# A layer-norm square root moved from GpSimd to ScalarE, V stores moved to GpSimd's queue, and unread matmuls in the gaps of an opening

## Chip, cores, metric

One core of a Trainium2 chip. The metric is the time of one execution in microseconds (us) on the device; each run is one execution. The core has a matmul engine (PE, with its weight loads PEld), VectorE (DVE), ScalarE (ACT), GpSimd (POOL) and SyncE (SP, which here only issues transfers). Runs come in two states, "fast" and "slow": on one core, a run is counted as slow when it took over 1.5% longer than the fastest run of the same kernel.

## The reference, cut to what matters

```python
def _attn_ref(q, k, v, sort_net):            # 4 batches, 8 heads, 768 rows, 64 columns
    P = sort_net
    for _ in range(5):                       # Sinkhorn: exp and two normalisations
        P = np.exp(P - np.max(P, axis=-1, keepdims=True))
        P = P / (np.sum(P, axis=-1, keepdims=True) + 1e-09)
        P = P / (np.sum(P, axis=-2, keepdims=True) + 1e-09)
    # (lines drawn together) ... keys and values mixed blockwise by P, then softmax attention in each block

def _moe_ref(x, w_ch1, w_ch2):
    mixed = np.real(np.fft.fft(np.fft.fft(x, axis=1), axis=2))
    u = x + mixed
    mu = np.mean(u, axis=-1, keepdims=True)
    var = np.mean((u - mu) ** 2, axis=-1, keepdims=True)
    un = (u - mu) / np.sqrt(var + 1e-06)     # the layer norm of this case
    return u + np.maximum(un @ w_ch1, 0.0) @ w_ch2
```

`x` is the attention output (4 x 768 x 512). Each batch is normalised in two halves of three 128-row tiles: eight normalisations in all.

## The kernel before

The program lists operations with estimated costs and lets a planner decide, before anything runs, in which order each engine takes them and which buffer each uses. So a cost that is wrong in the list gives a wrong order. The parts concerned:

```python
    many("u", 6, [128, DM], F32)
    many("un", 2, [128, DM], F16)
# ... mixed V to DRAM (SP) and back, spread differently (POOL)
                P.add({"SP": (0.4, 4.2)}, lambda _, w64=w64, cols=cols:
                      nc.sync.dma_start(vdr[t][w64, cols], vm[w64, cols]), ...)
                o = P.add({"POOL": (1.3, 1.3)}, ...  nc.gpsimd.dma_start(vsb..., vdr[t]...))
# ... the normalisation: mv holds mean and variance of three tiles
        P.add({"POOL": (0.25, 0.25)}, lambda _: G.tensor_scalar(
            mv.ap[:, :, 1], mv.ap[:, :, 1], 1e-6, None, op0=ALU.add), ...)
        P.add({"POOL": (0.9, 0.9)}, lambda _: G.tensor_tensor(
            ny.ap, mv.ap[:, :, 1], mhalf, op=ALU.pow), ...)          # (var+eps)^-0.5
        P.add({"POOL": (0.2, 0.2)}, ...)                             # nm = mean*ny
        P.add({"POOL": (0.25, 0.25)}, ...)                           # nm = -nm
# ... un = u*ny + nm, on ACT or DVE; batch 0 transposes it on PE, the others by DMA on SP
# ... first MLP layer: 4 matmuls fill a bank, ACT or DVE empties it with a relu into hr
            P.add({"ACT": act(GT), "DVE": dve(GT)}, f, r=[ps], w=[("h", g, fc)], ...)
# ... second layer into a bank; DVE adds it to u; u goes out
                    nc.gpsimd.indirect_dma_start(out..., rows[...], u.ap, None)
            P.add({"SP": (0.1, 2.3)} if g == 0 else {"POOL": (1.2, 3.5)}, f, ..., tag="out")
```

The output rows of the second half of a batch are scattered by a transfer that this kernel issues from GpSimd, and `u` has six buffers, so a later `u` can be written only when such a store has landed.

Names used below: `ex`, exponentials of the attention scores; `vdr`, mixed V in DRAM, and `vsf`, the same gathered back; `rt`, attention output; `rb`, a small operand of the Fourier products, brought in by four transfers on SP; `un` and `ut`, the normalised rows and their transpose; `hr`, an emptied bank of the first MLP layer ("bank" is one of the eight result buffers that the program sets up for PE; the MLP layers use three); `ny` and `nm`, the norm's factor and offset.

The softmax here doesn't subtract the row's maximum and nothing guards it: scores larger than these inputs give would overflow.

Of the kernel before, what the change touches and what calls it, by code (L numbers as in the profile page):

```python
# [25 lines left out]
RSC = 1.0 / XSC  # L26
YSC = 1.0 / 32.0
LOOK = {}
QB = (2, 3)
NK = 193  # L30
TOK = [list(range(1, 129)), list(range(129, 257)),
# [339 lines left out]
def kernel(  # L371
# [63 lines left out]
    many("y", 1, [128, 4, 2 * NK], F16)  # L435
    many("hi", 1, [128, 258], F16)
    many("u", 6, [128, DM], F32)
    many("un", 2, [128, DM], F16)
    many("ut", 2, [128, 4, GT], F16)
    tab = ct("tab", [128, 2, 2, 257], F32)  # L440
    cs = ct("cs", [128, 2, 3, 2 * NK], F16)
# [10 lines left out]
    vbn = ct("vbn", [128, D], F16)  # L452
    rows = ct("rows", [128, 3 * B], mybir.dt.uint32)
    negone = ct("negone", [128, 1], F32)
    mhalf = ct("mhalf", [128, 3], F32)
    mone = ct("mone", [128, 3], F32)
    many("rz", 4, [128, 6], F32)
    many("st", 3, [128, 6], F32)
    many("mv", 2, [128, 3, 2], F32)
# [23 lines left out]
    def load(dst, src, nbytes, w, prio, eng="POOL", r=(), after=()):  # L483
        e = {"POOL": nc.gpsimd, "SP": nc.sync}[eng]
        c = (0.8, 0.8) if eng == "POOL" else (0.1, 2.3)
        o = P.add({eng: c}, lambda _: e.dma_start(dst, src), r=r, w=w,  # L486
                  prio=prio, nbytes=nbytes, tag="load", after=after,
                  behind=gate)
        o.late = 4.0 if after else 0.0
        return o  # L490


    gate = ()
# [32 lines left out]
    def hk(g):  # L526
        return [("h", g, fc) for fc in range(16)]

    def load_v(t, hf, prio):
        if t == 0:  # L530
            load(nat[0][:, 3072 * hf:3072 * hf + 3072].rearrange(
                "p (c d) -> p c d", d=D),
                vv[0:128, 48 * hf:48 * hf + 48, :], 1572864,
                [("nat", 0, hf)] + hk(0)[8 * hf:8 * hf + 8], prio)
            return
        keys = kqk(2 * hf) + kqk(2 * hf + 1)
        past = {o for n in keys for d_ in (P.wr, P.rd) for o in d_.get(n, ())}
        for n in keys:
            P.wr[n], P.rd[n] = [], []
        for r in range(3 * hf, 3 * hf + 3):  # L540
            load(nat[1][:, 1024 * r:1024 * r + 1024].rearrange(
                "p (c d) -> p c d", d=D),
                vv[128:256].rearrange(
                    "p (c r) d -> p r c d", r=6)[:, r], 690000,
                [("nat", 1, r)], prio + 0.01 * r, after=tuple(past))
            P.ops[-1].late = 0.0
            for n in keys:
                P.wr[n].append(P.ops[-1])
# [16 lines left out]
    for n in range(2):  # L565
# [4 lines left out]
        vsb[0:96, :, D:D + 1], 1.0 / XSC), w=["vsz"], prio=-200.0, tag="vsz")  # L570
    P.add({"POOL": (0.1, 0.4)}, lambda _: nc.gpsimd.memset(
        pmt[:, 4:7, DM:DM + 2], 0.0), w=["pmz"], prio=-150.0, tag="small")
    for t_, val in ((negone, -1.0), (mhalf, -0.5), (mone, 1.0)):
        P.add({"POOL": (0.1, 0.4)}, lambda _, t_=t_, val=val:
              nc.gpsimd.memset(t_, val), w=["smalls"], prio=-199.0, tag="small")
    P.add({"POOL": (0.9, 0.9)}, lambda _: nc.gpsimd.tensor_tensor(
        mone, mone, mhalf, op=ALU.pow), r=["smalls"], w=["mone"], prio=-198.0,
        tag="small")

    early = dict(  # L580
        pw=(pw, sort_net.rearrange("b h i j -> (b h) i j"), 8192),
# [167 lines left out]
    def v_mix(t):  # L749
# [27 lines left out]
        for hb in range(2):  # L777
            w64 = slice(64 * hb, 64 * hb + 64)
            for k_ in range(3):
                cols = slice(2048 * k_, 2048 * k_ + 2048)  # L780
                P.add({"SP": (0.4, 4.2)}, lambda _, w64=w64, cols=cols:
                      nc.sync.dma_start(vdr[t][w64, cols], vm[w64, cols]),
                      r=[("vm", t, n) for n in range(4 * k_, 4 * k_ + 4)]
                      + (stage if t else vmk), w=[("vdr", t, k_, hb)],
                      prio=P.prio + 6 * hb, tag="vst")
# [401 lines left out]
    def dft2(b, g):  # L1187
# [11 lines left out]
        for tt in range(3):  # L1199
# [62 lines left out]
                mv.ap[:, tt, :], st.ap), r=[st], w=[(mv, tt)], tag="bna")  # L1262
        ny, nm = Buf("ny"), Buf("nm")
        mvs = [(mv, tt) for tt in range(3)]
        G = nc.gpsimd
        P.add({"POOL": (0.25, 0.25)}, lambda _: G.tensor_scalar(  # L1266
            mv.ap[:, :, 1], mv.ap[:, :, 1], 1e-6, None, op0=ALU.add),
            r=mvs, w=[(mv, 3)], tag="ln")
        P.add({"POOL": (0.9, 0.9)}, lambda _: G.tensor_tensor(
            ny.ap, mv.ap[:, :, 1], mhalf, op=ALU.pow),  # L1270
            r=[(mv, 3), "mone"], w=[ny], tag="ln")
        P.add({"POOL": (0.2, 0.2)}, lambda _: G.tensor_tensor(
            nm.ap, mv.ap[:, :, 0], ny.ap, op=ALU.mult),
            r=[(mv, 3), ny], w=[nm], tag="ln")
        P.add({"POOL": (0.25, 0.25)}, lambda _: G.tensor_scalar(
            nm.ap, nm.ap, -1.0, None, op0=ALU.mult), r=[nm], w=[(nm, 1)],
            tag="ln")
        lns.append(P.ops[-1])
        ut = Buf("ut")
        uts[b, g] = ut  # L1280
        for tt in range(3):
            un, pt, u = Buf("un"), Buf("pf"), us[b, g][tt]

            def f(e, tt=tt, un=un, u=u):
                if e == "ACT":
                    nc.scalar.activation(un.ap, u.ap, AF.Identity,  # L1286
                                         scale=ny.ap[:, tt:tt + 1],
                                         bias=nm.ap[:, tt:tt + 1])
                else:
                    V.tensor_scalar(un.ap, u.ap, ny.ap[:, tt:tt + 1],  # L1290
                                    nm.ap[:, tt:tt + 1],
                                    op0=ALU.mult, op1=ALU.add)
            P.add({"ACT": (0.72, 0.81), "DVE": (0.45, 0.55)}, f,
                  r=[u, ny, (nm, 1)], w=[un], tag="un")
            if b > 0:
                P.add({"SP": (1.3, 4.0)}, lambda _, tt=tt, un=un:
                      nc.sync.dma_start_transpose(
# [141 lines left out]
                -300.0)  # L1439
    with tc.manual_schedule():  # L1440
        P.aim(goal[0])
        for o in P.schedule():
            o.fn(o.eng)
# [1 line left out]
_INS = ['q', 'k', 'v', 'sort_net', 'moe_w_ch1', 'moe_w_ch2']  # L1445
# [26 lines left out]
```

## Time and profile before

| | before |
|---|---|
| median (runs) | 297.19 us (three, 296.29 to 297.81) |
| PE busy | 257.1 us, 88% |
| first MLP matmul | 66.48 us |
| PE between 150 and 250 us | busy all 100 us |
| longest waits of PE after the start | ex 2.6, u 2.5, gathered V 1.6 us |

In the views by line, each row names line, engine, operation and tiles; the brackets at the end of a row say how long the engine had stood idle before it, and who released it.

### The profile page before, as it was taken

The numbers are of one execution on the slowest core, as the hardware profiler recorded it, in microseconds if no ns is written. First come the engines' busy times: TensorE is split into PE (matmuls) and PEld (weight loads), VectorE is DVE, ScalarE is ACT, GpSimd is POOL, SyncE is SP. The second block draws the span as 40 slices with busy tenths as digits, with TensorE's granted clock in tenths as the row PEclk, the third lists the DMA queues.
The fourth block names the chain that finished last, engine by engine and source line by source line (L and its number), as shares of the span: only waits on it lengthen the run. The fifth ranks groups of instructions, "written<-read, shape, count | busy, mean of one in ns | idle before, by whom it ended". The sixth has DMA issues, their size and how long they took to land.

```text
span 293.2 us, 5526 instructions
## 1 busy us (share of the span) xinstructions
PE 257.1 (88%) x2124; PEld 146.9 (50%) x2124; DVE 173.9 (59%) x407; ACT 145.1 (49%) x307; POOL 84.8 (29%) x120
## 2 busy tenths in 40 slices
PE   0698697769999999696999999999999999999980
PEld 0255484465555464453557456456555545545530
DVE  6899879896999997384999452146124315310020
ACT  2289649666642586643697126327514505605400
POOL 8914843049730056830220001023000212200021
PEclk9999759987999999999999999999999999999997
DMA  7999999999996369999303011411311131141001
GB/s 128 202 203 287 217 229 173 213 209 141 164 173 122 80 162 221 170 144 153 92 22 57 2 72 36 56 72 50 56 72 37 36 56 72 36 92 36 0 36 72
DMA packets 56543, 32.60 MB, mean 111 GB/s; under 512 B 42842, under 2 KB 51560, under 8 KB 56516
## 3 DMA queue, kind: packets, MB, share of 16 engines
q0 software_dynamic: 36592, 21.46, 50.6%
q1 hardware_dynamic: 19926, 10.80, 16.8%
q8 instruction: 16, 0.26, 0.4%
q14 instruction: 9, 0.07, 0.1%
HBM read 32.12 MB, written 9.44 MB: 142 GB/s over the span
## 4 chain that ended last, share of the span: by engine, by line
PE 47%; DMA 3%; issue 1%; DVE 1%; POOLq 0%; DVEq 0%
PE bank L1326 21%; PE bank L1347 20%; DMA out_dram<-u,rows 3%; PE bank L1221 1%; PE bank L1133 1%; PE bank L1060 1%; PE bank L1225 1%; PE bank L1021 1%; POOLq L1467 0%; PE bank L966 0%; PE bank L1138 0%; PE bank L1209 0%; DVE u L1355 0%; DVE u L1245 0%; PE bank L1143 0%
## 5 line engine op out<-in xcount | busy, mean ns | idle before, releaser
L1326 PE MATMUL bank<-ut,w1sb 128*128 128x384 f16 x512 | 93.8, 330 | 3.0 <-DVE u L1355 2.8
L1338 ACT ACTIVATE hr<-bank 128x384 f16<-128x384 f32 x109 | 53.3, 490 | 71.1 <-PE bank L1326 70.4
L1347 PE MATMUL bank<-w2sb,hr 128*128 128x512 f16 x384 | 87.8, 379 | 0.0
L1326 PEld LDWEIGHTS <-w1sb 128*128 128x128 f16 x512 | 48.9, 99 | 38.0 <-issue 5.0
L1347 PEld LDWEIGHTS <-hr 128*128 128x128 f16 x384 | 36.9, 98 | 41.7 <-issue 0.2
L1355 DVE TENSOR_TENSOR u<-bank,u 128x512 f32<-128x512 f32 x24 | 16.5, 690 | 54.5 <-PE bank L1347 54.2
L1030 ACT ACTIVATE ex<-bank 96x384 f32<-96x384 f32 x64 | 28.4, 485 | 10.7 <-PE bank L1021 10.2
L1368 POOL DMA_INDIRECT out_dram<-u,rows x12 | 12.1, 1006 | 72.4 <-DVE u L1355 54.4
L1266 POOL TENSOR_SCALAR mv<-mv 128x3 f32<-128x3 f32 x8 | 1.9, 240 | 78.8 <-DVE mv L1261 75.7
L788 POOL DMA_DIRECT2D vsf<-vdr x12 | 13.0, 1088 | 34.8 <-DMA vdr<-kq 23.4
L1060 PE MATMUL bank<-vsf,eb 97*128 97x65 f16 x416 | 18.6, 206 | 2.6 <-DMA vsf<-vdr 1.6
L1060 PEld LDWEIGHTS <-eb 97*128 97x128 f16 x416 | 16.8, 107 | 5.2 <-issue 2.8
L1045 ACT ACTIVATE eb<-ex,negone 96x384 f16<-96x384 f32 x31 | 18.5, 613 | 0.3
L486 POOL DMA_DIRECT2D kq<-in_q_dram x20 | 16.4, 833 | 6.9 <-DMA kq<-in_k_dram 2.1
L1286 ACT ACTIVATE un<-u,nm,ny 128x512 f16<-128x512 f32 x15 | 12.2, 811 | 11.4 <-DMA ut<-un 9.1
L1076 DVE TENSOR_TENSOR rt<-bank,rz 128x384 f16<-128x384 f32 x32 | 17.2, 549 | 0.4
L1245 DVE SCALAR_TENSOR_TENSOR u<-rt,bank 128x510 f32<-128x510 f16 x12 | 8.1, 679 | 15.5 <-DMA out_dram<-u,rows 9.9
L1233 DVE SCALAR_TENSOR_TENSOR u<-rt,bank 128x512 f32<-128x512 f16 x12 | 8.0, 685 | 14.8 <-PE bank L1225 14.8
L1259 DVE BATCH_NORM_STATS2 st<-u 128x6 f32<-128x512 f32 x24 | 16.1, 682 | 0.2
L1021 PE MATMUL bank<-qt,ks 64*128 64x96 f16 x256 | 12.8, 213 | 3.7 <-ACT ex L1030 2.9
L966 PE MATMUL bank<-bdk,kq 128*64 128x128 f16 x192 | 10.6, 228 | 3.4 <-ACT ex L1030 1.5
L694 ACT CAST ks<-bank 128x384 f16<-128x384 f32 x18 | 8.2, 484 | 10.7 <-PE bank L966 10.6
(137 smaller groups left out, 317.3 us busy)
## 6 DMA issues: line engine op xcount, KB each, us to landing
kq<-in_k_dram POOLq DMA_DIRECT2D x8, 384.0 KB, 10.1
vsf<-vdr POOLq DMA_DIRECT2D x12, 256.0 KB, 6.9
w1sb<-in_moe_w_ch_dram POOLq DMA_DIRECT2D x4, 512.0 KB, 16.9
w2sb<-in_moe_w_ch_dram POOLq DMA_DIRECT2D x4, 512.0 KB, 19.3
out_dram<-u SPq DMA_DIRECT2D x8, 256.0 KB, 2.0
hr<-in_v_dram POOLq DMA_DIRECT2D x2, 768.0 KB, 9.4
kq<-in_q_dram POOLq DMA_DIRECT2D x4, 384.0 KB, 13.9
vdr<-hr SPq DMA_DIRECT2D x6, 256.0 KB, 5.0
```

Source lines behind the costliest of these rows:

```text
L486: o = P.add({eng: c}, lambda _: e.dma_start(dst, src), r=r, w=w, prio=prio, nbytes=nbytes, tag="load", after=after, behind=gate)
L788: nc.gpsimd.dma_start(vsb[32 * k_:32 * k_ + 32, w64, 0:D], vdr[t][w64, cols].rearrange("g (c d) -> c g d", d=D)),
L1021: nc.tensor.matmul(pss[h2].ap[:, BLK * j:BLK * j + BLK], ks.ap[rows, 4 * g + j, :], qt.ap[rows, c0:c0 + BLK])
L1030: nc.scalar.activation(ex.ap, pss[h2].ap[0:96, 0:384], AF.Exp, scale=SCALE),
L1045: nc.scalar.activation(ed, src, AF.Identity, bias=negone[0:96])
L1060: nc.tensor.matmul(po.ap[:, 65 * T:65 * T + 65], eb.ap[:, e0:e0 + 128], vsf[:, vi:vi + 65], start=(n == 0), stop=(n == len(WIN[T]) - 1), s ...
L1076: P.add({"DVE": (0.45, 0.56)}, lambda _: V.tensor_tensor(rt.ap[:, :, D * h:D * h + D], po3()[:, :, 0:D], rz.ap[:, :, None].broadcast_to([1 ...
L1259: P.add({"DVE": (0.6, 0.69)}, lambda _, u=u, st=st: V.bn_stats(st.ap, u.ap), r=[u], w=[st], tag="bn")
L1326: nc.tensor.matmul(ps.ap[:, 0:GT], w1sb[:, c, 128 * fc:128 * fc + 128], ut.ap[:, c, :], start=(c == 0), stop=(c == 3))
L1338: nc.scalar.activation(hr[g][:, fc, :], ps.ap[:, 0:GT], AF.Relu)
L1347: nc.tensor.matmul(ps.ap, hr[g][:, fc, 128 * tt:128 * tt + 128], w2sb[:, fc, :], start=(fc == 0), stop=(fc == 15))
L1355: V.tensor_tensor(u.ap, ps.ap, u.ap, op=ALU.add),
```

## The change

The intent: use ScalarE, idle half of the time, for the square root (ln, then exp of minus half of it), free GpSimd and give it the V stores that had stood on SP before the transposes, and keep PE's clock up (0.74 and 0.57 in the two stretches from 29.3 to 44 us before) by matmuls whose result nobody reads. Three parts.

Part A, unread matmuls, planned into gaps until the first layer norm:

```diff
+SPIN = 0.22
+    spin = Buf("pm")
+    P.add({"PE": (0.001, 0.001)}, lambda _: None, w=[spin], prio=-9000.0, tag="spin")
...
         for o in P.schedule():
+            if o.eng == "PE":
+                if o.start < goal[0].end:
+                    for _ in range(int((o.start - t - 0.05) / SPIN)):
+                        nc.tensor.matmul(spin.ap[:, 0:480], idh, pack.bitcast(F16))
+                t = max(t, o.start + o.costs["PE"][0])
             o.fn(o.eng)
```

Part B, stores and one more buffer:

```diff
-    many("un", 2, [128, DM], F16)
+    many("un", 3, [128, DM], F16)
...
-                P.add({"SP": (0.4, 4.2)}, lambda _, w64=w64, cols=cols:
-                      nc.sync.dma_start(vdr[t][w64, cols], vm[w64, cols]),
+                P.add({"POOL": (0.7, 4.5)} if t else {"SP": (0.4, 4.2)},
+                      lambda e, w64=w64, cols=cols:
+                      (nc.gpsimd if e == "POOL" else nc.sync).dma_start(
+                          vdr[t][w64, cols], vm[w64, cols]),
+                      behind=() if t or hb == 0 else gets[0, 0][-1:],
```

Part C, the norm:

```diff
+    P.add({"ACT": (1.5, 1.6)}, lambda _: nc.scalar.activation(
+        mone, eps, AF.Ln), r=["eps"], w=["mone"], prio=-9000.0, tag="small")
...
-        # four operations on POOL: add eps, pow, mult, negate
+        P.add({"ACT": (0.17, 0.24)}, lambda _: nc.scalar.activation(
+            ny.ap, mv.ap[:, :, 1], AF.Ln, bias=eps), ...)
+        P.add({"ACT": (0.17, 0.24)}, lambda _: nc.scalar.activation(
+            ny.ap, ny.ap, AF.Exp, scale=-0.5), ...)
+        P.add({"DVE": (0.08, 0.18)}, lambda _: V.scalar_tensor_tensor(
+            nm.ap, mv.ap[:, :, 0], -1.0, ny.ap, op0=ALU.mult, op1=ALU.mult), ...)
...
-                    V.tensor_scalar(un.ap, u.ap, ny..., nm..., op0=ALU.mult, op1=ALU.add)
+                    V.tensor_scalar(un.ap, u.ap, mv..., ny..., op0=ALU.subtract, op1=ALU.mult)
```

(One more line of the change, a longer assumed landing time of a V load, is left out here.)

More of the change, by code (lines that the diff above doesn't have):

```diff
@@ L454 @@
     negone = ct("negone", [128, 1], F32)
-    mhalf = ct("mhalf", [128, 3], F32)
-    mone = ct("mone", [128, 3], F32)
+    eps = ct("eps", [128, 1], F32)
+    mone = ct("mone", [128, 1], F32)
     many("rz", 4, [128, 6], F32)
@@ L490, in load @@
         return o
+    spin = Buf("pm")
+    P.add({"PE": (0.001, 0.001)}, lambda _: None, w=[spin], prio=-9000.0,
+          tag="spin")
     gate = ()
@@ L534, in load_v @@
                 [("nat", 0, hf)] + hk(0)[8 * hf:8 * hf + 8], prio)
+            P.ops[-1].late = 1.2
             return
@@ L572 @@
         pmt[:, 4:7, DM:DM + 2], 0.0), w=["pmz"], prio=-150.0, tag="small")
-    for t_, val in ((negone, -1.0), (mhalf, -0.5), (mone, 1.0)):
-        P.add({"POOL": (0.1, 0.4)}, lambda _, t_=t_, val=val:
-              nc.gpsimd.memset(t_, val), w=["smalls"], prio=-199.0, tag="small")
-    P.add({"POOL": (0.9, 0.9)}, lambda _: nc.gpsimd.tensor_tensor(
-        mone, mone, mhalf, op=ALU.pow), r=["smalls"], w=["mone"], prio=-198.0,
-        tag="small")
+    P.add({"DVE": (0.06, 0.12)}, lambda _: V.memset(eps, 1e-6), w=["eps"],
+          prio=-9100.0, tag="small")
+    P.add({"POOL": (0.1, 0.4)}, lambda _: nc.gpsimd.memset(negone, -1.0),
+          w=["smalls"], prio=-199.0, tag="small")
+    P.add({"ACT": (1.5, 1.6)}, lambda _: nc.scalar.activation(
+        mone, eps, AF.Ln), r=["eps"], w=["mone"], prio=-9000.0, tag="small")
     early = dict(
@@ L1264, in dft2 @@
         mvs = [(mv, tt) for tt in range(3)]
-        G = nc.gpsimd
-        P.add({"POOL": (0.25, 0.25)}, lambda _: G.tensor_scalar(
-            mv.ap[:, :, 1], mv.ap[:, :, 1], 1e-6, None, op0=ALU.add),
-            r=mvs, w=[(mv, 3)], tag="ln")
-        P.add({"POOL": (0.9, 0.9)}, lambda _: G.tensor_tensor(
-            ny.ap, mv.ap[:, :, 1], mhalf, op=ALU.pow),
-            r=[(mv, 3), "mone"], w=[ny], tag="ln")
-        P.add({"POOL": (0.2, 0.2)}, lambda _: G.tensor_tensor(
-            nm.ap, mv.ap[:, :, 0], ny.ap, op=ALU.mult),
-            r=[(mv, 3), ny], w=[nm], tag="ln")
-        P.add({"POOL": (0.25, 0.25)}, lambda _: G.tensor_scalar(
-            nm.ap, nm.ap, -1.0, None, op0=ALU.mult), r=[nm], w=[(nm, 1)],
-            tag="ln")
+        P.add({"ACT": (0.17, 0.24)}, lambda _: nc.scalar.activation(
+            ny.ap, mv.ap[:, :, 1], AF.Ln, bias=eps), r=mvs + ["eps"],
+            w=[(ny, 0)], tag="ln")
+        P.add({"ACT": (0.17, 0.24)}, lambda _: nc.scalar.activation(
+            ny.ap, ny.ap, AF.Exp, scale=-0.5), r=[(ny, 0)], w=[ny], tag="ln")
+        P.add({"DVE": (0.08, 0.18)}, lambda _: V.scalar_tensor_tensor(
+            nm.ap, mv.ap[:, :, 0], -1.0, ny.ap, op0=ALU.mult, op1=ALU.mult),
+            r=mvs + [ny], w=[nm], tag="ln")
         lns.append(P.ops[-1])
@@ L1289, in f @@
                 else:
-                    V.tensor_scalar(un.ap, u.ap, ny.ap[:, tt:tt + 1],
-                                    nm.ap[:, tt:tt + 1],
-                                    op0=ALU.mult, op1=ALU.add)
+                    V.tensor_scalar(un.ap, u.ap, mv.ap[:, tt, 0:1],
+                                    ny.ap[:, tt:tt + 1],
+                                    op0=ALU.subtract, op1=ALU.mult)
             P.add({"ACT": (0.72, 0.81), "DVE": (0.45, 0.55)}, f,
-                  r=[u, ny, (nm, 1)], w=[un], tag="un")
+                  r=[u, ny, nm] + mvs, w=[un], tag="un")
             if b > 0:
@@ L1441 @@
         P.aim(goal[0])
+        P.add({"PE": (0.001, 0.001)}, lambda _: None, r=[spin],
+              after=[goal[0]], prio=-2000.0, tag="spun")
+        t = 3.5
         for o in P.schedule():
+            if o.eng == "PE":
+                if o.start < goal[0].end:
+                    for _ in range(int((o.start - t - 0.05) / SPIN)):
+                        nc.tensor.matmul(
+                            spin.ap[:, 0:480], idh,
+                            pack.bitcast(F16))
+                t = max(t, o.start + o.costs["PE"][0])
             o.fn(o.eng)
```

## The prediction

> **What bounds the kernel now.** I read the page first: busy shares, then the 40 slices.
>
> ```profile
> PE 257.1 (88%) x2124; PEld 146.9 (50%) x2124; DVE 173.9 (59%) x407; ACT 145.1 (49%) x307; POOL 84.8 (29%) x120
> ...
> PE   0698697769999999696999999999999999999980
> ...
> PEclk9999759987999999999999999999999999999997
> ```
>
> PE sets the end from about 66 us on; before that the opening is a chain through DMA, DVE, ACT and PE. The PEclk row has two dips, in slices 5 to 6 and 9 to 10. The view by stretches gives them sizes:
>
> ```profile
> core 0: us, PE busy (x) PEld busy (x) DVE busy (x) ACT busy (x) POOL busy (x), PEclk, DMA share, GB/s
> 29.30:36.60 7.30, 4.39 (x78) 3.53 (x77) 5.91 (x14) 5.00 (x12) 6.57 (x10) 0.74 1.03 217
> 36.60:44.00 7.40, 7.40 (x109) 6.57 (x106) 5.39 (x18) 3.44 (x8) 3.51 (x6) 0.57 1.21 228
> 58.60:66.00 7.40, 4.93 (x96) 4.50 (x95) 7.26 (x26) 4.51 (x8) 3.06 (x8) 0.83 1.24 209
> 66.00:73.30 7.30, 7.30 (x71) 4.37 (x68) 5.09 (x12) 4.88 (x10) 7.08 (x7) 0.70 1.63 141
> 150.00:200.00 50.00, 50.00 (x387) 28.33 (x382) 26.30 (x65) 22.29 (x48) 6.37 (x11) 1.00 0.19 44
> 200.00:250.00 50.00, 50.00 (x284) 27.32 (x282) 17.85 (x38) 21.75 (x45) 6.19 (x11) 1.00 0.22 55
> ```
>
> The two last rows matter most: from 150 to 250 us PE is busy in all 100 us while ACT is busy in 44. There nothing can be gained by relieving POOL, and whatever stalls PE is added to the end in full. What PE still waits for is in its wait view, and the stall of 2.56 us at 119.6 us is explained by ACT's order of time:
>
> ```profile
> PE bank L1021 <- ACT ex L1030: 2.9, 3, 2.6
> PE bank L1326 <- DVE u L1355: 2.8, 2, 2.5
> ...
> 118.35 0.81 ACT L1286 ACTIVATE un<-u,nm,ny 128x512 f16<-128x512 f32 x1 [3.69 <-DMA ut<-un]
> ```
>
> ACT stood 3.69 us before the third normalised tile (only two "un" buffers), since the transposes that read the first two sat on SP behind six mixed-V stores (8.37 us on SP, from 101.63). The exponentials behind it came late, and PE with them. The second wait is another one: DVE cannot write "u" until an output store issued at 129.70 has landed at about 137.2.
>
> What is removed costs this on POOL, per normalisation (first one):
>
> ```profile
> 59.38 0.25 POOL L1266 TENSOR_SCALAR mv<-mv 128x3 f32<-128x3 f32 x1 [8.82 <-DVE mv L1261]
> 59.71 0.89 POOL L1269 TENSOR_TENSOR ny<-mv,mhalf 128x3 f32<-128x3 f32 x1
> 60.68 0.19 POOL L1272 TENSOR_TENSOR nm<-mv,ny 128x3 f32<-128x3 f32 x1
> 60.96 0.26 POOL L1275 TENSOR_SCALAR nm<-nm 128x3 f32<-128x3 f32 x1
> ```
>
> The last moment is in place on DVE at 59.27 and the normalisation on ACT and DVE starts at 61.25: 1.98 us of latency, and none of it on an engine that anybody needs. The price of its substitute is in the first line of ACT:
>
> ```profile
> 0.72 1.28 ACT L626 ACT_TABLE_LOAD   x1 [0.72 <-PEq L1456]
> 2.95 0.26 ACT L626 ACTIVATE rv<-rv 32x64 f32<-32x64 f32 x1 [0.94 <-DVE rv L623]
> ```
>
> [...] in the order of ACT's instructions a load stands before each ln and another before each exp[...]; 18 loads where there was one. No run shows it yet, but the order is fixed. [...] the first six 512-column matmuls took 2.72 us, the next six 1.46; and the clock is 0.50 in the views of 33 to 41 and 64 to 70 us, after stretches in which PE was about half busy (1.01 of 2.00 us in 31 to 33, 1.14 of 2.00 in 62 to 64). [...]
>
> **The change, part by part.**
>
> Part A, unread matmuls. I count 68 in PE's order, 480 columns each, 0.20 us at full clock (worked out from 512 columns in about 0.216 us in the mixing stage). 34 stand before the first real work and hide behind the loads of V. 19 stand between about 25 and 50 us, 15 around the first normalisation. They keep a bank of the three for the MLP until then, where it is hardly needed. If the clock stays up: from 34.9 to 43 us PE works at half clock (39 attention-times-V matmuls in 2.31 us against about 1.2 at full speed, the 16 fp32 ones in 2.83 against 1.59 later), but DVE is the other half of that chain; its waits on PE there are 0.41 + 0.56 + 0.97 us, so I take 2 us, not 4. In the second dip PE is filled from 66.05 to about 70.4, so half of 4.4 us, 2.2, is gained in full. At chances of 0.65 and 0.55, as real gaps are longer than planned ones: -1.3 and -1.2 us.
>
> Part B, third "un" buffer and stores off SP: the stall of 2.56 + 0.17 us should go; I take -2.2. In the first pair the stores of the first half now go ahead of those of the second half; the first attention matmul waited 1.59 us for the gather: -0.6. The second stall (2.5 us) depends on a store behind the loads of the last batch; the mixed-V stores join that queue, so I leave it at 0.
>
> Part C, ln and exp on ACT. Removed: 8 x 4 small operations on POOL, worth nothing in time. Added: 16 loads x 1.28 = 20.5 us, and 16 activations of about 0.25 = 4 us; ACT goes from 145 to about 170 us. The sum matters less than the place. The chain becomes load 1.28, ln 0.25, load 1.28, exp 0.25, a DVE operation of 0.2: 3.3 us with nothing hidden; the first load can run while ACT has nothing else, the second never can. While ACT sits in it, its evictions of MLP banks wait, and so do DVE's normalisations and the evictions behind them. Three banks of 0.65 us of matmul each are all PE can fill meanwhile. Worked through for the first half of batches 2 and 3 and the last normalisation (in all three the two loads stand together between evictions of the first MLP layer): a bank is full at 0; ACT evicts it until 0.6, then 0.6 + 1.28 + 0.25 + 1.28 + 0.25 = 3.65, next eviction done at 4.1. PE wants that bank at 2.6: 1.5 us of stall; the second layer's first bank is freed by DVE only at about 5.4 against 4.75: another 0.65. So about 2.1 us each, 6.3. The two others of batches 1 and 2 have work for other banks between the loads: about 1.5 each, 3.0. For the first half of batch 1 one load hides behind 1.6 us of fp32 matmuls: about 1.3. Sum 10.6; the order was packed with cheaper activations in mind and there is some slack that I can't see, so I count 8.5. For batch 0: un starts some 2.5 us later (63.75 against 61.25), but the third copy that the MLP waits for is then only about 1.1 us later, as before it waited for attention matmuls anyway: +1.1. At the very start an ln is put first, which leaves the wrong set loaded: the first exponential comes at about 4.25 instead of 2.95. Most of that 1.3 us is taken back where DVE's copy took 2.49 us alongside POOL's memsets: +0.4.
>
> Sum: -1.3 -1.2 -2.2 -0.6 +8.5 +1.1 +0.4 = +4.7; the time becomes 297.2 + 4.7, about 301.9. As the author's aim was speed and some of part B may reach further than I see, I shade it to 301.
>
> **The rivals.** (1) Loads hidden: ACT is idle half of the filled stage, so the loads fall into its idle time. Then C costs 2 or 3 us and the whole gives about 295. For it: 44 busy of 100 us. Against it: the order puts them right behind an eviction. (2) The clock is the prize: both dips vanish and the opening moves forward by 4 to 5 us, with B 7: then with C at 8.5 it is a draw at about 298, with C small 291. For it: the 0.50 clock over some 16 us. Against it: DVE is busy 7.26 of 7.40 us around the normalisation, and a chain longer than planned opens an idle gap that the planned matmuls do not fill. [...] (4) The stores on POOL's queue hold up gathers and loads of the last batch, and with them the output stores; DVE's wait for "u" grows by 1 to 3 us.
>
> **Range and chances.** C is the largest and is certain in its existence (18 loads), uncertain in its size from 3 to 20 us; A and B together -1 to -8. Low 293 (rival 1), high 309[...]. Faster by over 2% means under 291.2, which needs small stalls and all of A and B: 0.09. Slower means over 303.1: 0.36. Within 2%: 0.55.
>
> **What would show it.** Right: 18 table loads of about 1.28 us in ACT's groups; PE no longer busy in all of 150 to 250 us, with waits of its first MLP layer on ACT or DVE evictions of 1 to 2 us, one or two per normalisation, some 8 us in total; no 2.56 us wait on "ex"; PEclk without the first dip. Wrong: PE still filled after 150 us (then the loads hid), loads of another length or fewer of them, or the dips still at 0.5 (then A gave nothing). If B fails, ACT still waits for transposes before its third normalisation.

Passages marked as cut stated what no trace or run of this case shows; one of them is rival 3, near which the high end of 309 had been set. No term of the sum is among them: -1.3 -1.2 -2.2 -0.6 +8.5 +1.1 +0.4 = +4.7, from 297.2 to about 301.9, shaded to 301. The "about 1.2 at full speed" in Part A is an estimate; 39 of these matmuls took 1.35 us at 123.87 us in the trace of the kernel before, where the granted clock was 1.00. The "+0.4" in Part C supposed a second load at the start: the first profile of the changed kernel has loads at 0.74 and 2.88 us and the first Sinkhorn exponential at 4.17, and DVE's copy took 1.20 us there instead of 2.49.

## The result

The changed kernel took 313.68 us (median of four runs, 311.57 to 317.11), against 297.09 (296.29 to 297.81, four runs) for the kernel before in the same rounds. The ratio is 1.0535, 95% interval 1.0467 to 1.0604: slower by about 16 us, and over 4 us above the upper end of the prediction. All outputs were correct. Ratios in this document are the mean time of one kernel's fast runs over that of the other's fast runs of the same rounds, so not quite the ratio of the medians quoted.

The profile taken then fell in a slow run. The kernel was therefore profiled again (run i4 below: 314.88 us, ratio 1.0611, all six runs fast); the lines that follow are of that fast profile. Its busy shares, from the page:

```profile
PE 272.0 (87%) x2192; PEld 150.4 (48%) x2192; DVE 178.1 (57%) x426; ACT 163.0 (52%) x331; POOL 73.9 (24%) x91
```

PE has 68 matmuls more than before; ACT gained 18 us, POOL lost 11. The view by stretches, same columns as in the prediction:

```profile
29.30:36.60 7.30, 6.98 (x84) 4.54 (x79) 6.48 (x17) 6.35 (x15) 5.49 (x9) 0.90 1.03 216
36.60:44.00 7.40, 6.81 (x149) 5.76 (x149) 7.30 (x24) 4.94 (x13) 4.32 (x6) 1.00 1.20 259
...
58.60:66.00 7.40, 5.78 (x74) 3.23 (x71) 4.49 (x11) 6.15 (x12) 3.42 (x3) 0.80 1.21 206
...
150.00:200.00 50.00, 45.85 (x409) 26.01 (x408) 30.86 (x77) 30.46 (x63) 0.96 (x1) 1.00 0.15 39
200.00:250.00 50.00, 46.67 (x260) 24.93 (x258) 18.12 (x40) 23.57 (x46) 2.87 (x3) 1.00 0.16 48
```

The clock column of 29 to 44 us rose from 0.74 and 0.57 to 0.90 and 1.00: the unread matmuls did what they are for (the same stretches read 0.72 and 0.59 in f3 and 0.77 and 0.54 in e5, which have none, and 0.84 and 1.00 in e1 and f2, which have them). But the last two rows have lost their 50.00. PE now stands still for 7.5 us in that stretch. Whom it waits for, from PE's wait view:

```profile
PE bank L1330 <- DVE u L1359: 6.0, 1, 6.0
PE bank L1330 <- ACT hr L1342: 4.4, 3, 1.5
...
PE bank L1030 <- ACT ex L1039: 1.4, 2, 1.3
...
PE bank L1142 <- ACT y L1160: 1.2, 1, 1.2
PE bank L1351 <- DVE hr L1339: 1.2, 3, 0.4
PE bank L1330 <- DVE hr L1339: 1.1, 1, 1.1
```

The kernel before waited 2.5 us for `u` and 2.6 us for ex; the waits on `hr` and `y`, 4.4 + 1.2 + 1.2 + 1.1 = 7.9 us in these lines, are new: its PE was full from 150 us on. The wait for `u` grew from 2.5 to 6.0 us. Behind it stands a wait of DVE for an output store, 7.67 us where the kernel before had 4.20:

```profile
145.39 0.69 DVE L1254 SCALAR_TENSOR_TENSOR u<-rt,bank 128x510 f32<-128x510 f16 x1 [7.67 <-DMA out_dram<-u,rows]
```

How one of them comes about, in order of time (the first normalised half of batch 2; `hr` is an evicted MLP bank, the loads at L1274 and L1277 stand before ln and exp):

```profile
193.12 0.49 ACT L1342 ACTIVATE hr<-bank 128x384 f16<-128x384 f32 x1 [0.16 <-PE bank L1330]
193.63 1.28 ACT L1274 ACT_TABLE_LOAD   x1
194.92 0.30 ACT L1274 ACTIVATE ny<-mv,eps 128x3 f32<-128x3 f32 x1
195.24 1.28 ACT L1277 ACT_TABLE_LOAD   x1
...
196.64 0.47 ACT L1342 ACTIVATE hr<-bank 128x384 f16<-128x384 f32 x1
...
197.17 0.81 PE L1330 MATMUL bank<-ut,w1sb 128*128 128x384 f16 x4 [1.48 <-ACT hr L1342]
...
198.36 0.81 PE L1351 MATMUL bank<-w2sb,hr 128*128 128x512 f16 x3 [0.39 <-DVE hr L1339]
```

ACT empties a bank at 193.12 and the next only at 196.64, since two loads, ln and exp stand between; PE, out of banks, waits 1.48 us and then another 0.39. Exactly these two waits recur at 248.4 and 249.6, and at 272.5 and 273.7. Summed over the six normalisations of batches 1 to 3: 1.27 + 0.17, 1.21 + 0.75 + 0.19, 1.48 + 0.39, 1.12 + 0.34, 1.48 + 0.39 and 1.48 + 0.39, together 10.7 us.

The loads themselves, from the groups of ACT:

```profile
L1274 ACT ACT_TABLE_LOAD x8 | 10.3, 1283 | 0.1
L1277 ACT ACT_TABLE_LOAD x8 | 10.3, 1283 | 0.1
```

In the opening, the first normalisation of batch 0 on ACT (the fourth row is the first load of the second normalisation):

```profile
63.56 1.28 ACT L1274 ACT_TABLE_LOAD   x1
...
65.53 1.28 ACT L1277 ACT_TABLE_LOAD   x1
...
67.26 0.81 ACT L1290 ACTIVATE un<-u,nm,ny 128x512 f16<-128x512 f32 x1 [0.23 <-DVE nm L1279]
...
70.04 1.28 ACT L1274 ACT_TABLE_LOAD   x1
...
71.53 0.56 ACT L700 COPY ut<-bank 128x512 f16<-128x512 f16 x1
```

Two loads lie between the moments and the normalised tile, and a third one, belonging to the next normalisation, stands in front of the last copy (71.53) that the MLP needs. A copy for attention (`ks`, at 65.06, not shown) stands behind the first load, and attention matmuls wait for it, 0.20 us in e1 below and here 1.62:

```profile
65.57 0.55 PE L1069 MATMUL bank<-vsf,eb 97*128 97x65 f16 x13 [1.62 <-ACT ks L700]
```

The first MLP matmul starts at 72.84, before at 66.48.

### The profile page after: what moved, and what is told of

Same layout as the page of the kernel before. It is cut to its first block, busy times and chain, and to the rows that moved or that the text cites. A ratio compares the mean times of both kernels' runs of the same rounds, so it can differ in the third digit from the quotient of the medians.

```text
span 315.3 us, 5640 instructions
## 1 busy us (share of the span) xinstructions
PE 275.3 (87%) x2192; PEld 151.6 (48%) x2192; DVE 180.2 (57%) x426; ACT 163.3 (52%) x331; POOL 73.3 (23%) x91
## 4 chain that ended last, share of the span: by engine, by line
PE 40%; ACT 6%; DMA 4%; DVE 2%; issue 2%; POOLq 0%; DVEq 0%
PE bank L1351 19%; PE bank L1330 16%; DMA out_dram<-u,rows 4%; ACT L1274 2%; PE bank L1230 1%; PE bank L1069 1%; DVE un L1294 1%; ACT L1277 1%; ACT y L1160 1%; PE bank L1030 1%; PE bank L1234 1%; ACT hr L1342 1%; PE bank L1142 1%; ACT ny L1274 0%; DVE hr L1339 0%
## 5 line engine op out<-in xcount | busy, mean ns | idle before, releaser
L1330 PE MATMUL bank<-ut,w1sb 128*128 128x384 f16 x512 | 95.1, 331 | 12.2 <-DVE u L1359 6.5
L1342 ACT ACTIVATE hr<-bank 128x384 f16<-128x384 f32 x106 | 51.2, 489 | 88.4 <-PE bank L1330 88.1
L1351 PE MATMUL bank<-w2sb,hr 128*128 128x512 f16 x384 | 89.0, 382 | 1.5 <-DVE hr L1339 1.2
L1453 PE MATMUL bank<-pack 128*128 128x480 f16 x68 | 20.6, 436 | 3.3 <-DMA pack<-k_pack 3.3
L1054 ACT ACTIVATE eb<-ex,negone 96x384 f16<-96x384 f32 x34 | 20.3, 613 | 0.2
L1069 PE MATMUL bank<-vsf,eb 97*128 97x65 f16 x416 | 17.3, 197 | 3.1 <-ACT ks L700 1.6
L1069 PEld LDWEIGHTS <-eb 97*128 97x128 f16 x416 | 15.6, 100 | 6.6 <-issue 4.4
L1279 DVE SCALAR_TENSOR_TENSOR nm<-mv,ny 128x3 f32<-128x3 f32 x8 | 1.3, 162 | 20.7 <-ACT ny L1277 20.7
L1339 DVE TENSOR_SCALAR hr<-bank 128x384 f16<-128x384 f32 x22 | 12.1, 553 | 1.2 <-PE bank L1330 0.8
L1030 PEld LDWEIGHTS <-ks 64*128 64x128 f16 x256 | 7.4, 96 | 10.8 <-issue 9.6
```

The lines of the kernel that those rows point to most:

```text
L1030: nc.tensor.matmul(pss[h2].ap[:, BLK * j:BLK * j + BLK], ks.ap[rows, 4 * g + j, :], qt.ap[rows, c0:c0 + BLK])
L1054: nc.scalar.activation(ed, src, AF.Identity, bias=negone[0:96])
L1069: nc.tensor.matmul(po.ap[:, 65 * T:65 * T + 65], eb.ap[:, e0:e0 + 128], vsf[:, vi:vi + 65], start=(n == 0), stop=(n == len(WIN[T]) - 1), s ...
L1330: nc.tensor.matmul(ps.ap[:, 0:GT], w1sb[:, c, 128 * fc:128 * fc + 128], ut.ap[:, c, :], start=(c == 0), stop=(c == 3))
L1342: nc.scalar.activation(hr[g][:, fc, :], ps.ap[:, 0:GT], AF.Relu)
L1351: nc.tensor.matmul(ps.ap, hr[g][:, fc, 128 * tt:128 * tt + 128], w2sb[:, fc, :], start=(fc == 0), stop=(fc == 15))
```

## The experiments

17 kernels ran, all with correct outputs, in five groups, each beside runs of the kernel before on the same chip (the f and the g/h groups ran on one chip and share most of these).

| run | what it is | median us (runs) | before us (runs) | ratio of fast runs, 95% interval |
|---|---|---|---|---|
| e1 | change, one table load in all | 296.96 (4) | 297.63 (7) | 0.9989 [0.9905, 1.0073] |
| e2 | A and B, norm on POOL | 301.30 (4) | same | 1.0087 [1.0000, 1.0175] |
| e3 | C alone | 311.63 (4) | same | 1.0492 [1.0421, 1.0563] |
| e4 | A alone | 295.76 (4) | same | 0.9948 [0.9857, 1.0039] |
| f2 | e1 with stores on SP | 295.30 (4) | 299.31 (8) | 0.9849 [0.9783, 0.9916] |
| f3 | third un buffer alone | 296.43 (4) | same | 0.9831 [0.9749, 0.9913] |
| f4 | f2, second MLP weights held back | 295.06 (4) | same | 0.9833 [0.9773, 0.9894] |
| e5 | B alone | 299.52 (4) | same | 1.0019 [0.9946, 1.0092] |
| g1 | change, loads in batches 1 to 3 only | 309.76 (4) | 299.11 (9) | none given |
| g2 | change, loads in batch 0 only | 303.80 (4) | same | 1.0093 [0.9993, 1.0192] |
| h1 | A and third buffer, norm on POOL | 296.20 (4) | same | 0.9933 [0.9856, 1.0010] |
| h2 | f2, output store before last loads | 290.65 (4) | same | 0.9714 [0.9660, 0.9768] |
| i1 | third buffer and early output store | 293.45 (6) | 298.75 (11) | 0.9884 [0.9823, 0.9945] |
| i2 | i1 and A | 291.93 (6) | same | 0.9805 [0.9702, 0.9908] |
| i3 | h2 again | 291.14 (6) | same | 0.9805 [0.9743, 0.9868] |
| i4 | the change again | 314.88 (6) | same | 1.0611 [1.0548, 1.0674] |
| j1 | h2, half of the first MLP weights held too | 297.05 (5) | 297.38 (7) | 0.9936 [0.9868, 1.0004] |

**e1: take the loads away, leave everything else.** In the changed kernel a load stands before each ln and another before each exp; with the two at the start it has 18, of 1283 ns each. e1 asks once, at the start and by name, for one table set for both: its trace has one load (1283 ns). Nothing else moves: the order of instructions on each of the five engines is that of the changed kernel but for the loads.

```diff
+        nc.scalar.preload_act_table_set("natural_log_exp_and_others")
         nc.scalar.activation(mone, eps, AF.Ln)
```

> The changed kernel with one ACT table set that holds both ln and exp loaded at the start; the order of every engine is the same but for 17 of the 18 loads. Theory 1 (the loads set the loss): the five stalls of 1.0 to 2 us per normalisation after 110 us vanish (about 10.5 us in all), the opening gains about 3 to 5 us; time 296 to 300 us. Theory 2 (the new order sets it: the wait for u of 6.5 us, the wait for rb of 2.9 us, stores on POOL): the loads were mostly hidden and the time stays over 306 us.

296.96 us, ratio 0.9989. The loss is gone, all of it. In the stretch from 150 to 250 us PE is full again, and the first MLP matmul is back at 67.94:

```profile
150.00:200.00 50.00, 50.00 (x391) 27.96 (x389) 28.48 (x71) 21.27 (x49) 1.91 (x2) 1.00 0.16 45
```

In the opening, the same place on ACT in e1:

```profile
62.08 0.30 ACT L1277 ACTIVATE ny<-mv,eps 128x3 f32<-128x3 f32 x1
...
62.62 0.22 ACT L1280 ACTIVATE ny<-ny 128x3 f32<-128x3 f32 x1
63.07 0.81 ACT L1293 ACTIVATE un<-u,nm,ny 128x512 f16<-128x512 f32 x1 [0.23 <-DVE nm L1282]
```

From the start of the norm to the tile takes 1.0 us, with the two loads 3.7. So 17 loads, 21.8 us of ACT's time (17 x 1.283), cost about 16 us of the end. But e1 also shows that the rest of the change gains nothing that can be seen (its interval ends at 0.9905, 2.8 us), where the prediction had 5.3 us of gain. A new wait stands where the third buffer had removed one:

```profile
PE bank L1072 <- DMA vsf<-vdr: 4.5, 1, 4.5
```

**e2, e3, e4: the parts apart.** e2 is the change with Part C undone, e3 the kernel before with Part C, e4 the kernel before with Part A.

```diff
# e2, against the changed kernel
-        P.add({"ACT": ...}, ... AF.Ln ...); P.add({"ACT": ...}, ... AF.Exp ...)
+        P.add({"POOL": ...}, ... op=ALU.pow ...)   # the four POOL operations of before
# e3, against the kernel before: Part C's hunks; e4: Part A's hunks
```

> Unread matmuls, third un buffer and stores on POOL, but the normalisation on POOL as before. Theory 1: no loads, so 291 to 298 us, a gain of 0 to 6 us over before. Theory 2: still over 303 us, as the stores on POOL and the unread matmuls are what costs.

> The kernel before with ln and exp on ACT alone. Theory 1: 307 to 314 us, nearly the whole loss, with PE stalls of 1 to 2 us at each normalisation after 110 us. Theory 2: under 302 us.

> The kernel before with the unread matmuls alone. Prediction's step A: 294 to 296 us with the clock near 1.0 from 29 to 44 us. Theory 3 (the gain is swallowed, since the first Fourier product waits for the rb rows, which land at about 54 us whatever PE does): clock is up but the time stays at 296 to 298.5 us, with a PE wait on rb of 2 to 3 us.

C alone costs 1.0492, that is nearly the whole loss, with the same 18 loads of 1283 ns. A and B without C give 1.0087: no gain, rather a loss, where I had expected 291 to 298 us. A alone gives 0.9948, whose interval includes 1. With A the mean clock of the profiled run rose to 0.989 (0.963 before), yet the first Fourier product that needs `rb` waited 2.0 us for that transfer instead of 1.1: part of the clock's gain was waited away. Still the first MLP matmul came 2.5 us earlier (63.97 against 66.48), and the first eight matmuls of that layer took 1.47 us instead of 2.74. The end shows less of it: DVE's write of `u` came only 1.95 us earlier (135.32 against 137.27), after a wait of 6.02 us for an output store.

**g1 and g2: which loads cost what.** From e1, loads are put back by an explicit request before ln and before exp, in g1 for batches 1 to 3 (12 loads), in g2 for batch 0 (4 loads). Again each engine's order equals that of the changed kernel but for the loads.

```diff
         def f_ln(_):
+            if b > 0:            # g2: if b == 0
+                nc.scalar.preload_act_table_set("natural_log")
             nc.scalar.activation(ny.ap, mv.ap[:, :, 1], AF.Ln, bias=eps)
         def f_exp(_):
+            if b > 0:            # g2: if b == 0
+                nc.scalar.preload_act_table_set("natural_log_exp_and_others")
             nc.scalar.activation(ny.ap, ny.ap, AF.Exp, scale=-0.5)
```

> The changed kernel with no table load in the two normalisations of batch 0 and both loads in each of the six normalisations of batches 1 to 3; every engine's order is that of the changed kernel but for the loads. e1 (no such load) took 296.96 us and the changed kernel 313.68. Theory: the waits counted in the trace of the changed kernel from 150 us on, 10.5 us, are the price of these twelve loads: 306.5 to 308.5 us, ratio 1.035. Rival, from my shaded sum: 8.5 us, about 305.5 us. Second rival: nearly all of the loss is here, 312 us, and the opening costs only 1.1 us as predicted.

> The complement of g1: the four loads in the two normalisations of batch 0, none later. Theory: the loads hold up the first MLP chain by 5 to 6 us and with it the gathers, loads and the output store near 130 us, so the time is 297 plus 5 to 7, about 303 us, ratio 1.02; with g1 the two differences to e1 add up to the loss of 16.7 us within 2 us. Rival (my step of the prediction, plus 1.1): 298 us, ratio 1.003, and the two differences don't add up or g1 takes nearly all.

g1: 309.76 us. No ratio of fast runs was given for it: two of its four runs, 310.05 and 310.22, count as slow beside its own 305.01, though at nearly the same clock. By medians of all runs it is 309.76 over 299.11, 1.036; by its two fast runs (309.48 and 305.01) about 1.028. g2: 1.0093 by fast runs, 1.016 by medians; its interval touches 1. Against e1 (0.9989, another chip) that is 2.9 to 3.7% and 1.0 to 1.7%, 9 to 11 and 3 to 5 us; together 12 to 16, the changed kernel having lost 16 to 18 against e1. By medians the two parts add up; by fast runs about 4 us are missing. g1's rival of 8.5 us is not excluded by these times. That the opening costs more than the rival's 1.1 us is shown by the traces, not by g2's interval: the first MLP matmul is at 72.08 in g2 and 67.80 in g1, and the profiled execution of g2 (301.7 us) is 7.2 us longer than that of e1 (294.5).

**f3, e5, f2: the buffer and the stores.**

```diff
# f3 and e5, against the kernel before
+    many("un", 3, [128, DM], F16)
# e5 adds the store hunk of Part B; f2 takes its POOL part out of e1 again
# (the order of the first stores, "behind", stays as in the change):
-                P.add({"POOL": (0.7, 4.5)} if t else {"SP": (0.4, 4.2)},
+                P.add({"SP": (0.4, 4.2)},
```

> The kernel before with three un buffers instead of two, and nothing else. My step in part B: the ACT stall of 3.69 us and the PE wait of 2.6 us on ex go, the time falls by about 2.2 us to 295 us (ratio 0.992). Rival: a later wait (u on the output store, or the mixed-V gathers) takes the gain back and the ratio is 1.000 within 0.003.

> The kernel before with part B only: stores of pair 1 on POOL, stores of the first half of pair 0 first, three un buffers. Prediction's step: minus 2.8 us, 294.5 us, ratio 0.991. Theory after e1: the stores on POOL delay the gathers of pair 1, a PE wait of 2 to 5 us on vsf near 120 us appears, and the gain of the third buffer is lost: ratio 0.998 to 1.010. Compared with f3 of the same call it tells the stores apart from the buffer.

> The changed kernel with one table load (as e1) and the mixed-V stores of pair 1 back on the SP queue; what is left of the change is the third un buffer, the unread matmuls and ln and exp on ACT. Theory (the stores on POOL's queue stand ahead of the gathers of pair 1, so the V wait of 4.5 us in e1 is their price): that wait goes, un stays unstalled thanks to the third buffer, and the time is 293 to 295 us, ratio about 0.985. Rival (the wait belongs to the replanned order as a whole): some other wait of 2 to 4 us takes its place and the time stays at 297 us, ratio 0.995 to 1.0.

The third buffer alone gives 0.9831 (only two of its four runs are fast; by medians of all runs 0.990), with the stores on POOL 1.0019. In e1 against f2 the same difference appears, on two chips and with intervals that just touch: 0.9989 with the stores on POOL, 0.9849 without. So moving the stores costs 1 to 2%, roughly 3 to 5 us, twice, and takes back what the buffer gave. The wait on `vsf` falls from 4.5 us in e1 to 1.6 in f2; in e5 there is a wait of PE of 6.9 us on DVE's attention output `rt`, ending at 141.6 us, in its place. DVE writes that `rt` at 140.98, right after a `u` for which it waited on the same output store as in the changed kernel:

```profile
132.22 1.09 POOL L1371 DMA_INDIRECT out_dram<-u,rows  x1 [0.57 <-DVE rz L1076]
140.37 0.69 DVE L1248 SCALAR_TENSOR_TENSOR u<-rt,bank 128x510 f32<-128x510 f16 x1 [8.23 <-DMA out_dram<-u,rows]
```

POOL issues that store at 132.2 us in e5 and at 132.4 in e1, with the V stores on SP at 129.5 in f3 and 129.1 in f2: about 3 us later both times, the size of the loss. So the chain reads: stores and the gathers that read them stand in one queue and alternate on POOL from 100 to 118 us; two of the key and query loads behind them wait on the gathers (1.88 and 2.50 us in e5); the output store leaves late. It is read from traces; no run changed the order alone.

The traces also say why earlier gains fade. In nine profiles (before, e1, e4, e5, f2, f3, f4, g2, h1) the time from DVE's write of `u` after this store to the end is 155.4 to 158.2 us (e2, with 162.8, is an exception). What comes before counts only as far as it moves this write: in f3's profile (a slow run) the stall on ex is gone, but the wait on `u` is 4.9 us instead of 2.5, and the write stands at 137.12 against 137.27. With table loads in batches 1 to 3 the time after the write is 167.7 us (i4) and 169.1 (g1), 10 to 14 us more.

**f4 and j1: what holds up rb.** In the six profiles compared (before, the change, e4, f4, h2, j1) the first product with `rb` starts between 52.6 and 55.7 us. Issuing the transfers earlier helps less than it should: SP starts at 43.3 us in e4 and at 45.8 before, and the products start at 52.6 and 54.3. I suspected the large weight loads ahead of it.

```diff
# f4, against f2: w2 loads only after rb has landed
+    P.add({"POOL": (0.3, 0.4)}, lambda _: nc.gpsimd.tensor_copy(
+        w2sb[0:96, 0:16:4, 0:1], rb[0:96, 0:4][:, :, None]),
+        r=[("rb", n) for n in range(4)], w=[("w2", c) for c in range(4)], ...)
# j1, against h2: the same, and a second copy into half of w1sb
```

> f2 with one small POOL copy that makes the loads of the second MLP weights wait until the four rb transfers have landed (values are overwritten by the loads, so the result is right). Theory (the clock gained in the opening is swallowed since rb lands at 54 us whenever it is issued, its DMA engines being full of weight loads): the wait of the first Fourier product on rb falls from 3 to at most 1 us, and the time is 2 to 3 us under f2. Rival (rb waits for something else): rb wait unchanged within 0.5 us and the time within 0.3% of f2.

> h2 with half of the first MLP weights and all of the second ones issued only when the four rb transfers have landed. If weight loads ahead of them in the DMA engines hold rb up, the rb wait falls from 3.1 us to at most 1.5 us, whatever the total does. If the wait stays at 2.5 us or more, the weight loads are not the cause. The first MLP product needs these weights near 68 us and may wait for them, so the time may well be 1 to 5 us above h2.

Refuted twice. The held loads did leave late (from 55.5 us in f4 and 56.3 in j1), but the wait was 2.7 us in f4 and 3.6 in j1, against 3.4 in f2 and 3.1 in h2; f4's time equals f2's, and j1, on another chip, shows nothing of what h2 had won. What holds `rb` up stays open: in j1 the DMA engines were full until 54 us, but at a share of 0.11 from 54 to 56 us, and the product still started only at 55.7. Openings also differ from run to run: f3 and i1 below have the same order of instructions on every engine until 120 us, and their first products with `rb` start at 53.8 and 56.6 us (both profiles are of slow runs).

**h1, h2: what is left.** h1 is e4 with the third buffer. h2 goes at the wait for `u`, which is 3.6 us in f2. There, POOL's queue and DVE show (order of time, two engines):

```profile
127.07 1.75 POOL L487 DMA_DIRECT2D kq<-in_q_dram  x2 [1.59 <-ACT pmt L1118]
129.12 1.04 POOL L1375 DMA_INDIRECT out_dram<-u,rows  x1 [0.30 <-DVE rt L1088]
```

```profile
136.59 0.69 DVE L1257 SCALAR_TENSOR_TENSOR u<-rt,bank 128x510 f32<-128x510 f16 x1 [4.62 <-DMA out_dram<-u,rows]
```

The store is issued at 129.12 behind the last loads of keys and queries, and DVE writes the buffer it frees only at 136.59. h2 makes five of those loads wait for the store:

```diff
+            if (b, g) == (0, 1):
+                out1 = [o for o in P.ops[n0:] if o.tag == "out"][0]
+                for o in held:          # loads of k and q, batch 3, second half
+                    o.preds.add(out1)
```

> The kernel before with the unread matmuls and the third un buffer, normalisation on POOL as before and the stores on SP. f3 (buffer alone) was at 0.983, e4 (unread matmuls alone) at 0.995. If the two add: ratio 0.978. Rival (the clock gain is swallowed by rb, or the u wait grows and takes it): 0.983 to 0.99. Beside f2, which has ln and exp with one load instead: if h1 is equal to f2 (0.985) within 0.5%, the move of the norm from POOL to ACT is worth nothing without its loads.

> f2 with the last five loads of batch 3's keys and queries made to wait until the first scattered output store of batch 0 has been issued; this store then leaves POOL near 127.6 us instead of 129.1 and doesn't queue behind them. Theory (the u wait is the landing of that store behind loads in the DMA queue): the PE wait of 3.6 us on u falls below 1 us and the time is 2 to 3 us under f2, about 292.5 us, ratio 0.976. Rival (the loads are then needed later and another wait comes): 0.983 to 0.99.

In h2 the order on POOL is turned round:

```profile
127.18 1.10 POOL L1375 DMA_INDIRECT out_dram<-u,rows  x1 [6.14 <-DVE u L1362]
128.28 0.81 POOL L487 DMA_DIRECT2D kq<-in_k_dram  x1
```

DVE writes `u` at 130.86 without waiting, at most 3.7 us after the store's issue (127.18) where f2 took about 7.5 (129.12 to 136.59); PE's wait on it is gone, and the time is 290.65 us, ratio 0.9714: better than both kernels, and 4.6 us under f2 in medians on the same chip. From this write to the end it is 157.5 us, as in the other profiles. h1, at 0.9933, kept its 3.0 us of u wait and was less good than hoped; that it is behind f3 is within the intervals.

**i1 to i4: repeats and what A and C are worth then.** i1 is f3 with h2's edit, i2 is h1 with it, i3 and i4 are h2 and the changed kernel unaltered. i2 and i3 differ in the place of the norm and also, slightly, in the order of the first V stores.

```diff
# i1 against f3, i2 against h1: as h2
+                for o in held:
+                    o.preds.add(out1)
```

> The kernel before with the third un buffer and the last five loads of keys and queries behind the first scattered output store; no unread matmuls, normalisation on POOL, stores on SP. f3 was 0.983 with a u wait of 4.9 us; if the early store takes that wait away without a new one, 0.972 to 0.977. If the clock of the opening matters, this is 0.5% or more behind i2; if not, they are equal within 0.3%.

> As i1 with the unread matmuls. Prediction's step A (minus 2.5 us at chances, 4.2 in full): 0.5 to 1.4% under i1. Rival (the chain through DMA, rv and rb, and DVE sets the opening, and a warmer PE only waits longer): equal to i1 within 0.3%. Normalisation: if ln and exp with one load give something, i3 is under this; if not, equal within 0.3%.

> h2 again, letter for letter, in five rounds: 0.971 within 0.005, faster by over 2%. No u wait over 0.5 us, PE busy in all of 150 to 250 us.

> The changed kernel again, letter for letter: ratio 1.05 within 0.007. A fast profile is expected to show the same waits from 150 us on (1.2 to 1.5 us each, about 10 us in all) and the same 18 loads; if the waits there are under 7 us in a fast run, part of what I read was the state.

i4 confirms the loss (1.0611, above the 1.05 within 0.007 that I had written; 1.054 by medians) and, in a fast profile, the waits read from the slow one: expected about 10 us from 150 us on, found 9.2 (the 10.7 above without the 1.4 near 119 us). i3 repeats h2 at 0.9805, outside the 0.971 within 0.005 that I had written; the medians, 290.65 and 291.14, agree, but in i3's group the kernel before had five of eleven runs marked slow, and the ratio leaves those out. So h2 is 2 to 3% faster than the kernel before; "over 2%" is shown once and unclear once. i2 equals i3 (0.9805 both): with one load, ln and exp on ACT and the power on POOL cannot be told apart, within intervals of about 1%. i1 does not show the early store by ratios (0.9884 against 0.9831 of f3, two fast runs there; by medians 0.982 against 0.990); its profile does: the store is issued when it was in f3 (129.51 and 129.45 us) and lands about 3.4 us sooner, since the loads now stand behind it. i2 is below i1 by 2.5 us in fast means (293.1 and 290.6), as the prediction's step A says, but the intervals overlap and f3 against h1 points the other way; what A is worth stays open between nothing and 2.5 us.

## Why the prediction was wrong, point by point

The mechanism of the largest term, the table loads, was right. The steps that failed are sizes: the gain of A and B (-5.3 predicted, -0.3 in e1), the loads in the opening (+1.1, in the trace 3.4 to 4.9) and the loads in the filled stage (+8.5, in the trace 10.7).

1. **Part C in the filled stage: mechanism right, term mis-sized by its shading.** The worked sum over six normalisations was 10.6 us; the waits measured in the fast profile sum to 10.7 (single terms less well: about 2.1 was 1.87 three times, 1.5 was 2.15 and 1.46, 1.3 was 1.44). The step that failed is "there is some slack that I can't see, so I count 8.5". PE was full from 150 to 250 us, and the trace showed no slack to hide anything in. Cost: 2 us by the waits; the times of g1 (9 to 11 us) do not settle so small a difference.

2. **Part C in the opening, "+1.1".** This term was mis-sized the most. Against e1, which differs by the loads alone, the first MLP matmul is 4.9 us later in i4 (72.84 and 67.94), and 4.1 in g2. Some 1.5 us of the 4.9 arise before the norm begins (63.56 and 62.08; PE's mean clock from 58.6 to 66 us was 0.80 in i4 and 0.97 in e1). From the norm's start to that matmul it is 9.3 us in i4, 10.4 in g2 and 5.9 in e1: the loads cost 3.4 to 4.5. The two loads put off the normalised tile by 2.7 us, as predicted (2.5). The step that failed is that the third copy "waited for attention matmuls anyway", which was to swallow over half of it: in ACT's order a copy (`ks`, 65.06) stands behind the first load (63.56), so the attention matmuls themselves waited for it (1.62 us, in e1 0.20), and the load of the *second* normalisation stands in front of the third copy, 1.1 us more. The step "+0.4" for the first load before the Sinkhorn exp is not told apart by any run.

3. **Part B, "-2.2" and "-0.6": the stall went, the gain did not come.** The third buffer did remove the stall on ex. What that is worth stays between nothing and 1.7%: f3 gives 1 to 1.7%, but h1 (0.9933) is hardly better than e4 (0.9948), which it adds the buffer to. The "-0.6" cannot be seen: the first attention-times-V matmul starts at 36.4 us in e5 and 36.6 in i4, before at 34.9. The prediction left the stores at 0, with rival 4 (loads and with them output stores held up, the wait for `u` up by 1 to 3 us) outside the sum. Rival 4 came true: the output store left about 3 us later in e5 and e1, and DVE's wait for it is 8.23 us in e5 against 6.55 in f3, which differs by the stores (4.20 in the kernel before, where the stall on ex comes first). In e1 most of the delay shows as the wait for the gathers (4.5 us) instead, and DVE's is 3.05.

4. **Part A, "-1.3" and "-1.2".** Without C the opening went as predicted: the first MLP matmul starts at 63.97, 64.66 and 65.78 us in e4, h1 and i2, at 66.48, 66.16 and 68.95 in before, f3 and i1, 2.4 us on average, though openings scatter by as much. Of this e4's time keeps 1.5 us, in an interval that includes none, and the output store stands in between. In the changed kernel the first dip of the clock went, the second only came earlier (0.73 and 0.80 in the stretches from 51.3 to 66 us of i4; before, 0.83 and 0.70 from 58.6 to 73.3); there PE stood waiting for `rb`, 3.0 us in i4 against 1.05 before, and its mean clock from 51.3 to 58.6 us is that 0.73, before 1.00. (A small misreading: of the three waits of DVE on PE that the prediction adds up, the profile puts the 0.56 down to ACT.)

5. **The sum.** e1 stands for everything but the loads: a ratio of 0.9989, so -0.3 us in place of the -5.3 predicted for A and B. With 10.7 for the filled stage and 4.9 for the opening, 297.2 - 0.3 + 10.7 + 4.9 = 312.5 us, against 313.68 measured. Of the miss of 12.7 us, 5.0 are gains that did not come, about 3.8 the opening (4.9 for 1.1, clock and loads together), 2.2 the shading of the filled stage, 0.9 the last shading from 301.9 to 301, which had only the author's aim as its reason; the rest is unexplained. That the sum comes out so near is in part luck: from e1 to i4 the wait for the gathers (4.5 us) goes and the wait for `u` grows by as much (1.6 to 6.0), which is in no term of the sum. The two profiled executions differ by 18.6 us: 4.9 before the first MLP matmul, 11.8 of idle PE after it, 1.9 of longer PE work.

6. **What was right.** 18 loads of 1.28 us; no longer full from 150 us on; waits of 1 to 1.5 us, one or two for each normalisation; the order of ACT as the place to read them. Rival 1 (hidden loads) is refuted: between the two evictions around the loads at 193.63 and 195.24 lie 3.03 us, and two loads, ln and exp fill them (1.28 + 0.30 + 1.28 + 0.20). Nothing besides the load shows: the eviction before it ends at 193.61, the load ends at 194.91, and ln starts at 194.92.

## What to carry to other kernels

Here ln and exp cost what their table loads cost *at their place in ACT's order*: the bottleneck engine was full (PE busy in all 100 us from 150 to 250) and had three banks, and 12 loads (15.4 us) cost 9 to 11 us of the end (g1). So ask for one table set for both functions (e1: one load, 296.96 us against 313.68), or leave the function where it was. When a sum is worked out from the trace, don't shade it towards the author's hope. Before crediting an early gain, look for the next thing that all paths wait for: here an output store pinned the last 155 to 158 us. That wait was cured at the queue that issues the store: issue it before bulk loads that are needed later (f2 to h2: DVE's write of `u` at 130.86 us instead of 136.59, the median 4.6 us lower).
